# A narrow one-hot tile with its position innermost, and a bias on ScalarE in eight pieces, in an FFT and two-MoE kernel

## The chip, the cores and the metric

One core of a Trainium2 chip. The time is the device time of one execution in microseconds (us). The kernel before has a median of 3475.95 us over 3 runs.

## What is computed

The reference, cut to what matters:

```python
def reference(x, w_in, w_out, w_gate, w1, w2):
    X = np.fft.fft(np.fft.fft(x, axis=1), axis=2).real      # x: 8 x 3072 x 256
    x = X.reshape(24576, 256)
    h = x @ w_in                                            # 256 -> 2048
    x = np.where(h > 0, h, np.exp(np.minimum(h, 0)) - 1) @ w_out
    ...
    # second MoE: 24576 tokens, 8 experts, each takes exactly 3072 tokens:
    logits = x @ w_gate
    for idx in np.argsort(-logits.flatten()):               # greedy, best pair first
        tok, e = idx // 8, idx % 8
        if assigned[tok] >= 0 or counts[e] >= 3072: continue
        assigned[tok] = e; counts[e] += 1
    ...
    for e in range(8):
        out[mask_e] = np.maximum(x[mask_e] @ w1[e], 0) @ w2[e]   # 256 -> 1024 -> 256
```

## The kernel before, in words

The program has two parts. The first, `moe1`, makes the spectrum, the first MoE and the logits; it fills somewhat more than the first half of the time and the change doesn't touch it. The second, `moe2`, begins near 2000 us. It finds the order in which experts fill up, one expert after the other, and for each one does three things.

- `select(i)` finds the i-th expert to fill and the tokens that it takes, by a search over bits of the keys of the logits (lines 284 to 306) and then by counting (lines 327 to 386). A token is kept as a place: partition p of 128 and column j of 192 (NJ). The result is `ui`, the rank of each chosen token in the expert's list, which lines 393 to 401 split into `rb` (rank modulo 128) and `qb` (rank divided by 128, 0 to 23). Line 405 then adds a row of constants `cc` to all logits `L` (128 x 192 x 8), very negative for the expert that is full, and lines 408 and 409 mark its tokens as assigned. The first step of the next expert's selection, line 260, reads `L`.
- `listing(i)` turns ranks into a list of token numbers. It goes through the 192 columns in 12 pieces of 16. For a piece it makes two one-hot tiles in bf16: `oh` (line 479), 128 x 128 x 16, which is 1 where `rb` equals a given remainder; and the narrow `oq`, 128 x 48 x 16, in two halves: positions 24 to 47 are 1 where `qb` equals a given quotient (line 473), positions 0 to 23 are that times the column number (line 474), and then the upper half is scaled in place by the partition number (line 475, on ScalarE). In both tiles the column of the piece is innermost. `place` (line 452) then runs 16 matmuls, one for each column, with `oh[:, :, j]` as weights and `oq[:, :, j]` as the moving operand, so both are read with a step of 16 elements, and adds 16 results in PSUM. For experts 1 to 7 the sum is moved out after each piece (lines 457, 459); for expert 0 all 192 matmuls add into one PSUM tile, read at line 497. Line 498 makes the token numbers `idx`, and with these the rows of tokens are gathered from DRAM (line 522, on POOL's queue).
- `expert(i)` computes the expert: six groups of 512 tokens, each transposed (531), multiplied by w1 (553), split in a high and a low part on ScalarE and VectorE (565, 571), multiplied by w2 (594 to 596) and scattered (604).

The engine names are PE (TensorE), DVE (VectorE), ACT (ScalarE) and POOL (GpSimd). Each engine runs its instructions in the order in which they are written. That order comes from `ready` and from a loop that interleaves generators: while `expert(i)` is written out, steps of the next expert's `listing` and `select` are put between its matmuls, by a simple account of each engine's time (`pe`, `act`, `dve`). So for experts 1 to 7 the search and the list lie beside the previous expert's matmuls. For the first expert nothing lies beside them: `ready(0)` writes its steps in a fixed order, and there line 405 and line 474 run on POOL, where for later experts both run on DVE.

For expert 0 the tiles of the pieces come from the pool that the experts use later, so that they take no place of their own: `oh` alternates between the buffers `yh` and `yl`, the twelve `oq` are `hh0` to `hh5` and `hl0` to `hl5`. For experts 1 to 7 `oh` and `oq` have two buffers each.

Of the kernel before, what the change touches and what calls it, by code (L numbers as in the profile page):

```python
# [161 lines left out]
def moe2(tc, yd, R, w1, w2, out):  # L162
# [5 lines left out]
    with ExitStack() as ctx:  # L168
# [85 lines left out]
        def after():  # L254
            return max(ck.dve, ck.act) + AF0

        def select(i):
# [130 lines left out]
            yield after()  # L388
            while i - 1 in st and not st[i - 1]["listed"]:
                yield None  # L390
            ri = rt.tile([128, NJ], I32, name="ri")
            qi = rt.tile([128, NJ], I32, name="qi")
            nc.vector.tensor_scalar(ri, ui, 127, None, op0=OP.bitwise_and)
            nc.vector.tensor_scalar(qi, ui, 7, None, op0=OP.arith_shift_right)
# [7 lines left out]
            st[i] = dict(rb=rb, qb=qb, wix=wix, listed=False)  # L402
            dve(900)
            yield after()
            (nc.vector if i else nc.gpsimd).tensor_tensor(L, L, cc.unsqueeze(1).to_broadcast([128, NJ, E]), op=OP.add)
            dve(1700)
            yield after()
            nc.vector.scalar_tensor_tensor(u2, ui, float(CAP), fa, op0=OP.is_lt, op1=OP.mult)
            nc.vector.tensor_tensor(asg, asg, u2, op=OP.add)
            dve(600)  # L410
# [2 lines left out]
        def listing(i):  # L413
            while i not in st:
                yield None
            rb, qb, wix = (st[i][n] for n in ("rb", "qb", "wix"))
            wr = [wp.tile([128, 2 * FE], F32, name="wr%d" % a) for a in range(2)]
            for a, src in enumerate((w1.rearrange("e (p c) f -> (e p) (c f)", c=2),
                                     w2.rearrange("e (p c) d -> (e p) (c d)", c=8))):
                nc.gpsimd.indirect_dma_start(out=wr[a], out_offset=None, in_=src,  # L420
                                             in_offset=bass.IndirectOffsetOnAxis(ap=wix[:, 0:1], axis=0))
            fetched = ck.pe
            pj = small("pj", 48)
            prev = None
            while now[0] < i - 1:
                yield None
            wsp = [wp.tile([128, 2 * FE], F32R, name=n, bufs=2) for n in ("w1h", "w1l", "w2h", "w2l")]

            def split():
                for c in range(2):  # L430
                    rv = wr[0].rearrange("p (c f k) -> p c k f", c=2, k=8)[:, c]
                    hv, lv = (t.rearrange("p (c k f) -> p c k f", c=2, k=8)[:, c] for t in wsp[0:2])
                    nc.scalar.activation(hv, rv, AF.Copy)
                    (nc.gpsimd if i else nc.vector).tensor_tensor(lv, rv, hv, op=OP.subtract)
                    act(950)
                    yield after()
                for c in range(2):
                    ws = slice(1024 * c, 1024 * c + 1024)
                    nc.scalar.activation(wsp[2][:, ws], wr[1][:, ws], AF.Copy)
                    nc.gpsimd.tensor_tensor(wsp[3][:, ws], wr[1][:, ws], wsp[2][:, ws], op=OP.subtract)  # L440
                    act(950)
                    yield after()

            parts = split()

            if i == 0:
                pl0 = psum.tile([128, 48], F32, name="acc20")

            def place(c, oh, oq):
                pl = rps([128, 48]) if i else pl0  # L450
                for j in range(16):
                    nc.tensor.matmul(pl, oh[:, :, j], oq[:, :, j], start=j == 0 and (i > 0 or c == 0),  # L452
                                     stop=j == 15 and (i > 0 or c == NC - 1))
                if i == 0:
                    return
                if c:
                    nc.vector.tensor_tensor(pj, pl, pj, op=OP.add)
                else:
                    nc.vector.tensor_copy(pj, pl)

            for c in range(NC):
                js = slice(16 * c, 16 * c + 16)
                if i:
                    oh = rt.tile([128, 128, 16], BF16, name="oh", bufs=2)
                    oq = rt.tile([128, 48, 16], BF16, name="oq", bufs=2)
                else:
                    oh = ex.tile([128, 128, 16], BF16, name=("yh", "yl")[c % 2])
                    oq = ex.tile([128, 48, 16], BF16, name="h%s%d" % ("hl"[c % 2], c // 2), bufs=1)

                def row(a, n):  # L470
                    return a[:, js].unsqueeze(1).to_broadcast([128, n, 16])

                nc.vector.tensor_tensor(oq[:, 24:48], io16[:, 0:24], row(qb, 24), op=OP.is_equal)
                (nc.vector if i > 0 else nc.gpsimd).tensor_tensor(oq[:, 0:24], oq[:, 24:48], row(jb, 24), op=OP.mult)
                nc.scalar.activation(oq[:, 24:48], oq[:, 24:48], AF.Copy, scale=pcol)
                dve(750)
                act(450)
                yield 0
                nc.vector.tensor_tensor(oh, io16, row(rb, 128), op=OP.is_equal)
                if prev:  # L480
                    place(*prev)
                prev = (c, oh, oq)
                dve(1300)
                if ck.pe > fetched + WAIT:
                    next(parts, None)
                yield after()
            place(*prev)
            while ck.pe < fetched + WAIT and i and not draining[0]:
                yield None
            if i:  # L490
                yield from parts
            st[i]["listed"] = True
            while now[0] < i - 1:
                yield None
            idx = small("idx", 24, I32)
            if i == 0:
                nc.vector.tensor_copy(pj, pl0)
            nc.vector.scalar_tensor_tensor(idx, pj[:, 0:24], 128.0, pj[:, 24:48], op0=OP.mult, op1=OP.add)
            plan[i] = dict(idx=idx, wr=wr)
            plan[i]["w"] = wsp  # L500
            if i:
                ahead()
            else:
                fetch(*queue.pop(0))
                out_y[0] += 1
            dve(100)
            yield after()
            yield from parts
# [128 lines left out]
        def ready(i):  # L637
            draining[0] = True
            while i not in st:
                sel_s.step()  # L640
            if i == 0:
                for _ in range(5):
                    lst_s.step()
                sel_s.step()
            while i not in plan or "w" not in plan[i]:
                lst_s.step()
            if i == 0:
                for _ in range(1):
                    sel_s.step()
                for _ in range(2):  # L650
                    lst_s.step()
                for _ in range(2):
                    sel_s.step()
                turn(0, 0)
                for _ in range(2):
                    lst_s.step()
            draining[0] = False
            ck.pe = max(ck.pe, ck.dve - 1500)
            ahead()
# [634 lines left out]
```

## Time and profile before

| | |
|---|---|
| median of 3 runs | 3475.95 us (3472.55 to 3478.8) |
| profiled execution | 3493.99 us, of which the span is 3492.2 us |
| mean granted clock of TensorE | 0.977 of full speed |
| PE busy | 3343.3 us (96%) |
| DVE busy | 2637.7 us (76%) |
| ACT busy | 2257.5 us (65%) |
| POOL busy | 641.0 us (18%) |
| place of the first expert's list | about 2068 to 2100 us |

The span runs from the first to the last instruction of one profiled execution. That execution is 18 us longer than the median of the runs shown. Busy shares are averages over stages that have different limits. A row of a timeline gives start, duration, engine, line, operation, tiles (out<-in) and shapes; "x16" merges neighbouring instructions of one line, and the duration is then that of all of them. In brackets stands the idle time before it and what ended it.

### The profile page before, as it was taken

What the parts mean: (1) busy time and instruction counts of PE and PEld (TensorE: products, weight loads), DVE (VectorE), ACT (ScalarE), POOL (GpSimd) and SP (SyncE); (2) the same over time, 40 slices, a digit from 0 to 9 for tenths busy, and PEclk for the clock granted to TensorE, in tenths of its full rate; (3) what the DMA queues carried; (4) which work ended last, traced back from release to release, by engine and by line L of the source; (5) the groups of instructions that cost most, each with busy time, mean ns of one, the idle gap of its engine ahead of it and who ended that gap; (6) DMA issues with size and microseconds to landing.
All of it is one profiled execution on the core that took longest, in us unless ns stands there. A gap on an engine that the chain in (4) does not pass through costs nothing.

```text
span 3492.2 us, 62331 instructions
## 1 busy us (share of the span) xinstructions
PE 3343.3 (96%) x25472; PEld 3121.3 (89%) x25472; DVE 2637.7 (76%) x4930; ACT 2257.5 (65%) x3029; POOL 641.0 (18%) x837
## 2 busy tenths in 40 slices
PE   7999999999999999999999828999999999999999
PEld 4999999999999999999999827888798888888998
DVE  7888888888878888888878887677677777777522
ACT  4777777778777777777777736454546364645332
POOL 4000000000000000000000034333343334243432
PEclk9999999999999999999999958999999999999999
DMA  7112121121121111211100001111111111111110
GB/s 202 30 47 50 45 42 31 52 42 40 33 45 51 35 42 40 42 46 36 37 13 13 19 25 43 49 48 51 40 55 43 52 43 61 61 37 60 40 48 32
DMA packets 97075, 159.30 MB, mean 46 GB/s; under 512 B 18515, under 2 KB 68439, under 8 KB 94613
## 3 DMA queue, kind: packets, MB, share of 16 engines
q1 hardware_dynamic: 68357, 66.54, 7.8%
q0 software_dynamic: 24736, 80.42, 7.5%
q10 hardware_dynamic: 3696, 8.36, 0.7%
q8 instruction: 200, 3.28, 0.4%
q14 instruction: 86, 0.70, 0.1%
HBM read 91.78 MB, written 63.47 MB: 44 GB/s over the span
## 4 chain that ended last, share of the span: by engine, by line
PE 85%; DVE 6%; ACT 4%; issue 2%; DMA 1%; POOL 0%; another core or an unknown queue 0%; ACTq 0%; DVEq 0%; POOLq 0%; SPq 0%
PE hps L553 14%; PE acc L1116 11%; PE acc L1115 11%; PE acc L1114 11%; PE pq L1061 5%; PE pq L1063 5%; PE pq L1062 5%; PE acc L594 4%; PE acc L596 3%; PE acc L595 3%; PE rps L452 3%; ACT junk L289 3%; PE pq L1065 3%; PE pq L785 2%; PE pq L867 1%
## 5 line engine op out<-in xcount | busy, mean ns | idle before, releaser
L1116 PE MATMUL acc<-woh,gl 128*128 128x264 f32 x3072 | 876.1, 285 | 1.2 <-DVE gl L1101 1.1
L1115 PE MATMUL acc<-wol,gh 128*128 128x264 f32 x3072 | 875.2, 285 | 0.0
L1114 PE MATMUL acc<-woh,gh 128*128 128x264 f32 x3072 | 873.8, 284 | 1.3 <-DVE wol L1035 1.3
L1114 PEld LDWEIGHTS acc<-woh,gh 128*128 128x128 f32 x3072 | 578.9, 188 | 1.5 <-issue 1.5
L1116 PEld LDWEIGHTS acc<-woh,gl 128*128 128x128 f32 x3072 | 578.7, 188 | 1.7 <-DVE gl L1101 1.6
L1115 PEld LDWEIGHTS acc<-wol,gh 128*128 128x128 f32 x3072 | 577.8, 188 | 0.0
L1084 ACT ACTIVATE e<-h 128x1024 f32<-128x1024 f32 x384 | 408.5, 1064 | 158.5 <-DVE h L1078 158.1
L1077 DVE TENSOR_TENSOR h<-pq,qs 128x512 f32<-128x512 f32 x384 | 265.6, 692 | 287.9 <-ACT qs L1071 286.9
L1101 DVE TENSOR_TENSOR gl<-g,gh 128x1024 fp32r<-128x1024 f32 x384 | 468.4, 1220 | 1.6 <-ACT gh L1096 1.6
L1091 DVE SCALAR_TENSOR_TENSOR g<-e,h 128x1024 f32<-128x1024 f32 x384 | 467.5, 1218 | 0.1
L594 PE MATMUL acc<-w2h,hh 128*128 128x256 f32 x1536 | 455.9, 297 | 0.5 <-issue 0.4
L596 PE MATMUL acc<-w2h,hl 128*128 128x256 f32 x1536 | 435.0, 283 | 2.2 <-DVE hl L571 1.9
L595 PE MATMUL acc<-w2l,hh 128*128 128x256 f32 x1536 | 435.7, 284 | 0.0
L571 DVE SCALAR_TENSOR_TENSOR hl<-hps,hh 128x512 fp32r<-128x512 f32 x384 | 262.9, 688 | 216.6 <-ACT hh L565 195.8
L1086 ACT ACTIVATE e<-e 128x1024 f32<-128x1024 f32 x384 | 408.0, 1063 | 10.7
L1096 ACT ACTIVATE gh<-g 128x1024 fp32r<-128x1024 f32 x384 | 404.3, 1053 | 2.1 <-PE acc L1115 2.1
L1071 ACT ACTIVATE qs<-pq 128x512 f32<-128x512 f32 x384 | 230.2, 600 | 209.0 <-PE pq L1065 204.7
L565 ACT ACTIVATE hh<-hps 128x512 fp32r<-128x512 f32 x384 | 227.0, 594 | 200.1 <-PE hps L553 149.1
L604 POOL DMA_INDIRECT out<-osb,yg x192 | 203.6, 1060 | 621.6 <-ACT osb L601 591.5
L553 PE MATMUL hps<-yh,w1h 128*128 128x512 f32 x768 | 311.6, 406 | 2.0 <-DVE hl L571 1.9
L553 PE MATMUL hps<-yh,w1l 128*128 128x512 f32 x768 | 302.3, 394 | 0.0
L553 PE MATMUL hps<-yl,w1h 128*128 128x512 f32 x768 | 301.0, 392 | 0.0
(319 smaller groups left out, 7465.3 us busy)
## 6 DMA issues: line engine op xcount, KB each, us to landing
yd<-ysb SPq DMA_DIRECT2D x48, 514.0 KB
zd<-zev SPq DMA_DIRECT2D x29, 385.5 KB
xa<-x SPq DMA_DIRECT2D x28, 384.0 KB
zt<-zd SPq DMA_DIRECT2D x16, 193.5 KB
xa<-w_out ACTq DMA_DIRECT2D x6, 512.0 KB
zt<-zd SPq DMA_DIRECT2D x32, 96.0 KB
yg<-yd,idx POOLq DMA_INDIRECT x192
out<-osb,yg POOLq DMA_INDIRECT x192
```

Source lines behind the costliest of these rows:

```text
L553: nc.tensor.matmul(ps, w[:, ws], v[:, c], start=c + k == 0, stop=c + k == 3)
L594: nc.tensor.matmul(acc[t // 2][:, t % 2], hh[:, ts], w2h[:, fs], start=f == 0, stop=False)
L595: nc.tensor.matmul(acc[t // 2][:, t % 2], hh[:, ts], w2l[:, fs], start=False, stop=False)
L596: nc.tensor.matmul(acc[t // 2][:, t % 2], hl[:, ts], w2h[:, fs], start=False, stop=f == 7)
L1084: nc.scalar.activation(e, st["h"], AF.Relu, scale=-1.0)
L1086: nc.scalar.activation(st["e"], st["e"], AF.Exp, scale=-1.0)
L1091: nc.vector.scalar_tensor_tensor(g, st["e"], -1.0, st["h"], op0=OP.add, op1=OP.max)
L1096: nc.scalar.activation(st["gh"], st["g"], AF.Copy)
L1101: nc.vector.tensor_tensor(st["gl"], st["g"], st["gh"], op=OP.subtract)
L1114: nc.tensor.matmul(o, st["gh"][:, i, ts], woh(c), start=c == 0, stop=False)
L1115: nc.tensor.matmul(o, st["gh"][:, i, ts], wol(c), start=False, stop=False)
L1116: nc.tensor.matmul(o, st["gl"][:, i, ts], woh(c), start=False, stop=c == 15)
```

## The change

```diff
@@ select(i)
-            ri = rt.tile([128, NJ], I32, name="ri")
+            ri = rt.tile([128, NJ], I32, name="u1")
...
-            (nc.vector if i else nc.gpsimd).tensor_tensor(L, L, cc.unsqueeze(1).to_broadcast([128, NJ, E]), op=OP.add)
-            dve(1700)
-            yield after()
+            if i:
+                nc.vector.tensor_tensor(L, L, cc.unsqueeze(1).to_broadcast([128, NJ, E]), op=OP.add)
+                dve(1700)
+                yield after()
+            else:
+                for e in range(E):
+                    nc.scalar.activation(L[:, :, e], L[:, :, e], AF.Identity, bias=cc[:, e:e + 1])
+                    yield 0
@@ listing(i), place
-                    nc.tensor.matmul(pl, oh[:, :, j], oq[:, :, j], start=j == 0 and (i > 0 or c == 0),
+                    nc.tensor.matmul(pl, oh[:, :, j], oq[:, j], start=j == 0 and (i > 0 or c == 0),
@@ listing(i), the loop over 12 pieces
-                    oq = rt.tile([128, 48, 16], BF16, name="oq", bufs=2)
+                    oq = rt.tile([128, 16, 48], BF16, name="oq", bufs=2)
...
-                    oq = ex.tile([128, 48, 16], BF16, name="h%s%d" % ("hl"[c % 2], c // 2), bufs=1)
+                    oq = ex.tile([128, 16, 48], BF16, name="h%s%d" % ("hl"[c % 2], c // 2), bufs=1)
...
-                nc.vector.tensor_tensor(oq[:, 24:48], io16[:, 0:24], row(qb, 24), op=OP.is_equal)
-                (nc.vector if i > 0 else nc.gpsimd).tensor_tensor(oq[:, 0:24], oq[:, 24:48], row(jb, 24), op=OP.mult)
-                nc.scalar.activation(oq[:, 24:48], oq[:, 24:48], AF.Copy, scale=pcol)
+                eqq = (rt.tile([128, 24, 16], BF16, name="eqq") if i else
+                       ex.tile([128, 24, 16], BF16, name="hl7", bufs=1))
+                ov = oq.rearrange("p j q -> p q j")
+                nc.vector.tensor_tensor(eqq, io16[:, 0:24], row(qb, 24), op=OP.is_equal)
+                (nc.vector if i > 0 else nc.gpsimd).tensor_tensor(ov[:, 0:24], eqq, row(jb, 24), op=OP.mult)
+                nc.scalar.activation(ov[:, 24:48], eqq, AF.Copy, scale=pcol)
@@ ready(0)
-                for _ in range(5):
-                    lst_s.step()
-                sel_s.step()
+                for k in range(E):
+                    for _ in range(2):
+                        lst_s.step()
+                    sel_s.step()
```

The narrow tile becomes 128 x 16 x 48: the position is innermost, and the moving operand `oq[:, j]` of a matmul is 48 elements in a row. The comparison no longer goes into the tile itself but into a tile `eqq` of one buffer (`hl7` of the experts' pool for expert 0, so order rows of expert 0 call it `hl`), and the multiply and the scaling both read it and write into `oq` with a step of 48 elements. `oh` stays as it was. For expert 0 the addition to the logits leaves POOL and becomes eight activations on ACT, one for each expert's column of the logits, written one after each of the first eight pieces. `ri` shares the buffer of `u1`.

In the changed file the lines are 481 (comparison), 482 (multiply), 483 (scaling), 487 (`oh`), 457 (matmul) and 411 (the new activation).

DVE's order in the first expert's list, with the engines that each instruction waits for in brackets. Before:

```order
L473 TENSOR_TENSOR hh_24162<-io_23598,qb 128x384 [waits DMAHW1_49,DMAHW7_49,DMAHW0_49,DVE_49]
L479 TENSOR_TENSOR yh<-io_23598,rb 128x2048 [waits Activation_49]
L473 TENSOR_TENSOR hl_24168<-io_23598,qb 128x384
L479 TENSOR_TENSOR yl<-io_23598,rb 128x2048
L473 TENSOR_TENSOR hh_24190<-io_23598,qb 128x384
```

Changed:

```order
L481 TENSOR_TENSOR hl_24163<-io_23598,qb 128x384 [waits DMAHW1_49,DMAHW7_49,DMAHW0_49,DVE_49]
L487 TENSOR_TENSOR yh<-io_23598,rb 128x2048 [waits Activation_49]
L481 TENSOR_TENSOR hl_24171<-io_23598,qb 128x384 [waits Activation_49,Pool_49]
L487 TENSOR_TENSOR yl<-io_23598,rb 128x2048
L481 TENSOR_TENSOR hl_24195<-io_23598,qb 128x384 [waits Activation_49,Pool_49]
```

The order is the same; from the second piece on the comparison waits for ACT and POOL, which read `eqq` of the piece before.

ACT's order at the same place. Before:

```order
L400 ACTIVATE rb<-ri 128x192 [waits DVE_49]
L475 ACTIVATE hh_24162<-hh_24162,pcol 128x384 [waits DMAHW3_49,DMAHW1_49,DMAHW7_49,DMAHW0_49,Pool_49]
L475 ACTIVATE hl_24168<-hl_24168,pcol 128x384 [waits Pool_49]
L475 ACTIVATE hh_24190<-hh_24190,pcol 128x384 [waits Pool_49]
L475 ACTIVATE hl_24213<-hl_24213,pcol 128x384 [waits Pool_49]
```

Changed:

```order
L400 ACTIVATE rb<-u_24143 128x192 [waits DVE_49]
L483 ACTIVATE hh_24162<-hl_24163,pcol 128x24x16 [waits DMAHW3_49,DMAHW1_49,DMAHW7_49,DMAHW0_49,DVE_49]
L411 ACTIVATE L<-L,cc 128x192 [waits DMAHW3_49]
L483 ACTIVATE hl_24170<-hl_24171,pcol 128x24x16 [waits DVE_49]
L411 ACTIVATE L<-L,cc 128x192
```

The scaling waits for DVE's comparison and no longer for POOL's multiply, and between the scalings of the first eight pieces stand the eight additions to the logits. On POOL line 405, which stood between the third and the fourth multiply, is gone.

DVE's order in the lists of experts 1 to 7. Before:

```order
L473 TENSOR_TENSOR oq<-io_23598,qb 128x384 [waits DVE_49]
L474 TENSOR_TENSOR oq<-oq,jb 128x384 [waits DVE_49]
L479 TENSOR_TENSOR oh<-io_23598,rb 128x2048
L473 TENSOR_TENSOR oq<-io_23598,qb 128x384
L474 TENSOR_TENSOR oq<-oq,jb 128x384 [waits DVE_49]
```

Changed:

```order
L481 TENSOR_TENSOR eqq<-io_23598,qb 128x384 [waits DVE_49]
L482 TENSOR_TENSOR oq<-eqq,jb 128x24x16 [waits DVE_49]
L487 TENSOR_TENSOR oh<-io_23598,rb 128x2048
L481 TENSOR_TENSOR eqq<-io_23598,qb 128x384 [waits DVE_49,Activation_49]
L482 TENSOR_TENSOR oq<-eqq,jb 128x24x16 [waits DVE_49]
```

Here too the order stays, and the comparison of the second piece waits for ACT's scaling of the first. On PE the order of all instructions is the same in both kernels.

## Rows read from the trace of the kernel before

**Rows 1.** The page, busy time, share and instructions of each engine

```profile
PE 3343.3 (96%) x25472; PEld 3121.3 (89%) x25472; DVE 2637.7 (76%) x4930; ACT 2257.5 (65%) x3029; POOL 641.0 (18%) x837
```

**Rows 2.** By stretch: busy PE, PEld, DVE, ACT, POOL, granted clock, DMA, GB/s

```profile
2068.00:2100.00 32.00, 20.39 (x192) 19.00 (x192) 28.62 (x28) 10.03 (x14) 25.67 (x14) 0.50 0.09 32
2550.00:2630.00 80.00, 79.96 (x593) 72.04 (x593) 59.45 (x113) 35.22 (x53) 34.29 (x35) 1.00 0.17 56
```

**Rows 3.** The same for line 452 alone: busy PE, PEld, clock, DMA, GB/s

```profile
2550.00:2630.00 80.00, 20.75 (x192) 18.25 (x192) 1.00 0.17 56
```

**Rows 4.** Line 452: count: duration ns min/median/max, first and last start, forms

```profile
L452 PEld LDWEIGHTS <-oh x1344: 142/148/180, 2216.4 to 3278.4; 128*128 128x128 bf16 x192
L452 PE MATMUL rps<-oq,oh x1344: 267/279/306, 2216.4 to 3278.5; 128*128 128x48 bf16 x192
L452 PE MATMUL acc<-hh,yh x96: 255/279/288, 2070.7 to 2096.7; 128*128 128x48 bf16 x96
L452 PE MATMUL acc<-hl,yl x96: 255/278/288, 2072.8 to 2098.9; 128*128 128x48 bf16 x96
```

**Rows 5.** Timeline of PE, a run of 16 in the list of expert 2

```profile
2399.49 1.74 PE L452 MATMUL rps<-oq,oh 128*128 128x48 bf16 x16
```

**Rows 6.** Contiguous bf16 operands, lines 342, 376: by source, then timeline of PE

```profile
L342 PEld LDWEIGHTS <-gm x96: 95/96/106, 2060.4 to 3206.4; 128*128 128x128 bf16 x96
L342 PE MATMUL rps<-wb,gm x96: 169/169/183, 2062.5 to 3206.4; 128*128 128x16 bf16 x96
...
L376 PE MATMUL rps<-trij,tots x32: 243/245/368, 2064.9 to 3210.5; 96*128 96x192 bf16 x32
...
2199.56 0.44 PE L342 MATMUL rps<-wb,gm 128*128 128x16 bf16 x12 [0.28 <-DVE sgn L335]
```

**Rows 7.** First list, one run: timeline of PE, then line 452 by stretch

```profile
2095.30 1.70 PE L452 MATMUL acc<-hh,yh 128*128 128x48 bf16 x16 [0.44 <-ACT hh L475]
...
2095.29:2095.37 0.08, 0.07 (x1) 0.07 (x1) 0.50 0.00 0
2095.29:2095.38 0.09, 0.08 (x2) 0.08 (x2) 0.50 0.00 0
```

**Rows 8.** Timeline of DVE and of POOL, first pieces of the first list

```profile
2067.74 0.36 DVE L473 TENSOR_TENSOR hh<-io,qb 128x384 bf16<-128x384 bf16 x1
2068.02 1.22 DVE L479 TENSOR_TENSOR yh<-io,rb 128x2048 bf16<-128x2048 bf16 x1
2069.16 1.07 DVE L473 TENSOR_TENSOR hl<-io,qb 128x384 bf16<-128x384 bf16 x1
2071.28 1.07 DVE L473 TENSOR_TENSOR hh<-io,qb 128x384 bf16<-128x384 bf16 x1
...
2068.24 1.76 POOL L474 TENSOR_TENSOR hh<-hh,jb 128x384 bf16<-128x384 bf16 x1 [2.74 <-ACT rb L400]
```

**Rows 9.** The same around line 405, POOL and then DVE

```profile
2074.23 3.59 POOL L405 TENSOR_TENSOR L<-L,cc 128x1536 f32<-128x1536 f32 x1
...
2074.41 4.49 DVE L479 TENSOR_TENSOR yl<-io,rb 128x2048 bf16<-128x2048 bf16 x1
```

**Rows 10.** Line 400, an activation of 192 elements

```profile
L400 ACT ACTIVATE rb<-ri x1: 364/364/364, 2067.3 to 2067.3; 128x192 bf16<-128x192 int32 x1
```

**Rows 11.** End of the first list: timeline of POOL, ACT and PE

```profile
2094.89 1.84 POOL L474 TENSOR_TENSOR hl<-hl,jb 128x384 bf16<-128x384 bf16 x1 [0.29 <-DVE hl L473]
...
2096.76 0.62 ACT L475 ACTIVATE hl<-hl,pcol 128x384 bf16<-128x384 bf16 x1 [1.52 <-POOL hl L474]
...
2097.43 1.72 PE L452 MATMUL acc<-hl,yl 128*128 128x48 bf16 x16 [0.43 <-ACT hl L475]
```

**Rows 12.** Line 474 on DVE, experts 1 to 7

```profile
L474 DVE TENSOR_TENSOR oq<-oq,jb x84: 357/358/3140, 2214.8 to 3270.8; 128x384 bf16<-128x384 bf16 x84
```

**Rows 13.** Timeline of ACT and DVE, first two pieces of expert 1

```profile
2215.21 0.62 ACT L475 ACTIVATE oq<-oq,pcol 128x384 bf16<-128x384 bf16 x1 [2.75 <-DVE oq L474]
...
2216.23 0.35 DVE L473 TENSOR_TENSOR oq<-io,qb 128x384 bf16<-128x384 bf16 x1
```

## The prediction

> **What bounds the kernel now.** I read the totals first. TensorE (PE) is busy 96% of the span and VectorE (DVE) 76% [rows 1], but an average over stages prices no change, so next I cut the span around the lines that the change touches. They stand in two stages with different limits. In the 32 us in which the list of the first expert is made, PE is busy 20 us at a granted clock of 0.50, the lower of its two levels (1.2 GHz), while DVE is busy 28.6 and POOL 25.7 [rows 2]: a chain of DVE and POOL sets the time there. In a stretch in which a later expert's list is made, PE is busy 79.96 of 80 us at the full clock, DVE 59 of 80 [rows 2]: there PE alone sets the time, and of those 80 us the placing matmuls of line 452 take 20.75 [rows 3]. So what the new tile does for PE counts seven times, for experts 1 to 7, and what it does elsewhere counts once.
>
> **The placing matmuls.** There are 1344 in those seven lists (84 runs of 16) and 192 for the first expert [rows 4]. One run of 16 takes 1.74 us; less the 0.28 of the last matmul, and over 15 spacings, that is 97 ns from one to the next [rows 4, 5]. Is it the 48 moving columns or the 128 weight columns that cost this? Both are read with a step of 16 elements, and the change makes only the moving side contiguous.
>
> The moving side: matmuls with contiguous bf16 operands take 169 ns for 16 columns, 244 to 245 for 192 [rows 6], so some 163 plus 0.42 per column; 48 columns would take 183. The shortest of line 452 take 255 [rows 4]. They stand in the first expert's list, where PE waits for ACT before each run, so that the first matmul of a run finds its weights loaded: this is no wait for weights. So 48 stepped columns cost about 92 ns beyond the fixed 163, some 1.9 ns each, close to the spacing of 97. And the spacing is 97 at either level of the clock (1.70 and 1.74 us per run [rows 5, 7]). I take it that the moving read sets the spacing.
>
> The weight side, which stays: a stepped load takes 148 ns, a contiguous one of the same size 96 [rows 4, 6], so 52 ns more. Contiguous pairs follow each other at (0.44 - 0.169) / 11 = 25 ns [rows 6]; with the 52 on top a pair whose weights alone are stepped would take 77. A second reading comes from the start of a run in the first list, where the first matmul has its weights and the second waits for a stepped load that begins with the first: the second begins 70 to 80 ns later, since one has begun by 2095.37 and two by 2095.38 [rows 7]. I take 74 for the new spacing. The gain is 97 - 74 = 23 ns, and 23 x 1344 = 30.9 us, on PE's own path. Ends: 0 if the weight load needs all of the 97, and (97 - 25) x 1344 = 97 us if a stepped load hides as a contiguous one does.
>
> By the Trainium skill (TensorE: Matmul & The Clock Gate, section LDWEIGHTS) a weight load takes its columns over 1.2 ns, so 107 ns for 128; by that rule the load would keep the spacing where it is and this term would be zero. The rows speak against it, since pairs with 128 weight columns follow each other every 25 ns [rows 6]; it stays as a rival.
>
> **The first expert's list.** Today a piece runs thus [rows 8]: DVE compares (line 473, 0.36 us when nothing disturbs it), then makes the wide tile (479, 1.21); POOL's multiply (474) begins at 2068.24 and ends at 2070.00, and all but about 0.78 of it lies beside the end of line 479; the next compare, issued at 2069.16, ends 0.23 after POOL. DVE and POOL hold each other up here, and a piece takes 2.12 to 2.13 us (2069.16 to 2071.28).
> - *Line 405 leaves POOL.* It takes 3.59, and line 479 beside it takes 4.49 in place of 1.21 [rows 9]. Gain 3.3 us.
> - *Eight ScalarE pieces come.* An activation of 192 elements takes 0.36 [rows 10]. ACT is busy 10 of 32 us in this stage [rows 2], idle for 22, and nobody in the list waits for them: the reader of the logits, line 260, comes after the list. Cost 0, covered by that idle time; without that cover 8 x 0.36 = 2.9.
> - *DVE's compare now waits for POOL and ACT*, because there is one tile eqq. It already ended after POOL; now it starts after POOL. A piece becomes 0.28 (compare to wide tile) + 1.21 + 0.78 + about 0.06 for the signal = 2.33, so 0.20 more, 11 times: 2.2 us lost. Behind it on DVE stands the wide tile, for which PE waits.
> - *POOL now writes with a step of 96 bytes.* No row shows this. Lower end 0, since nothing suggests a gain. Line 405, of four-byte elements, takes 3.59 / 1536 = 2.3 ns each, line 474 about 0.78 / 384 = 2.0. I take this difference, 0.12 per piece, 1.4 us in all, as that row is nearest; upper end, an extra for each element as large as PE's stepped read, 384 x 1.9 ns = 0.73 per piece, 8.8 in all.
> - *The end of the list.* Today the last multiply, ACT's 0.62 and PE's 1.72 follow in series [rows 11]. ACT now reads eqq and not POOL's result, so its 0.65 with the signal goes, and the last run of 16 shortens by 15 x 0.023 plus about 0.08 of its last matmul. Gain 1.1.
>
> Sum of this stage: -3.3 + 2.2 + 1.4 - 1.1 = -0.8 us.
>
> The Trainium skill (GPSIMD Engine Reference, section Performance pitfalls for Q7 kernels) has a price for stepped reads only, about half more per element; if a stepped write paid as much, POOL would cost 0.39 x 12 = 4.7 us here, and the stage would come to +2.5.
>
> **Experts 1 to 7, beside PE.** DVE's multiply takes 0.36 for 384 elements [rows 12]; no row shows it with a stepped write. Lower end 0 more, upper end the same 0.73 more: 84 x 0.73 = 61 us over seven stretches, 9 in each, in which DVE has 20 of 80 us idle [rows 2]. Cost 0; without that cover DVE would reach PE's level and the gain would go. The new wait of the compare for ACT: I set the end of each ACT scaling (0.62) against the start of the next compare. The smallest distances are about 0.40, as in [rows 13]; of 77 only three are under 1 us. Cost 0, covered by these distances. Without them hl of the experts (line 571), which stands behind the compare on DVE, would be late, and PE waits for hl. Moving ri into u1's tile costs nothing: DVE writes and reads both in its own order, and u1's last reader comes before ri.
>
> **Sum.** -30.9 - 0.8 = -31.7 us against the profiled execution, whose time is 3494.0: 3462.3. The runs shown have a median of 3476.0, 18 us lower, so for the median I forecast 3476 - 31.7 = 3444 us.
>
> **The rivals.**
> - *The weight load sets the spacing, and the new tile gives PE nothing.* For it: the load is stepped too and lasts 148 ns. Against it: the 255 ns of matmuls that had their weights. It is where the rule on weight loads of the Trainium skill's page named above would lead. The time would be 3476 - 0.8 = 3475. Chance 0.14.
> - *The stepped load hides better than I take it.* For it: its excess may be latency. At a spacing of 43 ns, between 25 and 60, the gain is 54 x 1344 = 73 us, time 3402. Chance 0.18.
> - *The gain is partly given back*: DVE's multiply with a stepped write delays hl, for which PE waits. With half the gain gone, 3460. Against it: those 20 idle us in 80. Chance 0.06.
> - *Slower: POOL's stepped write* in the first list. Each microsecond more per piece costs 12 us, with nothing beside it. To lose 7 us in all against my other terms, it must take 0.9 + (31.7 + 7) / 12 = 4.1 us in place of 0.8, over 10 ns an element; at 5 us the time is 3476 - 31.7 + 49 = 3493. For it: the whole of POOL's step lies on the path there. Against it: nothing in the rows comes near that price. Chance 0.03.
>
> **How the numbers follow.** My forecast, spacings of 60 to 90 ns, has the remaining 0.59; it covers 3426 to 3466. The second rival reaches to 3402 and below; I let the range begin at 3404 and end at 3475, which leaves out half of that rival, part of the first and the last one, about 2 in 10. A measurement here can tell some 0.2%, 7 us, from no change. Faster by more than that: the forecast, the second and third rival, and 0.02 of the first, 0.85. Same: 0.12. Slower: 0.03.
>
> **What would show it.** Right: runs of 16 placing matmuls of about 1.3 us with matmul durations near or below 255 ns and weight loads still near 148; no POOL operation over the logits and no wide tile of 4.5 us; pieces of the first list of about 2.4 us; no wait of PE that is new in experts 1 to 7. A spacing still at 97 with short matmuls proves the weights to be the limit; pieces of 3 us or more, POOL's write.

## The result and the profile after

The changed kernel takes 3523.07 us (median of 4 runs, 3522.60 to 3528.39) against 3476.59 for the kernel before beside it: a ratio of 1.0138 (95% interval 1.0121 to 1.0156), 46.5 us slower. The forecast was 3444, faster; the time lies above its whole range.

Sets of runs differ a little: the kernel before takes 3475 to 3477 us in three of the four sets used here and 3491 in one, about the gap between the profiled execution and the median ahead of the prediction. What makes this difference isn't known; the record gives the same chip number to the set of 3491 and to one of the others. So spans are subtracted only between profiles of one set, and the sets are compared by their ratios to the kernel before. The rows below are from such a pair (`before_here` and `after_again` among the experiments): spans 3475.0 and 3517.5, 42.5 us apart.

The page of the changed kernel, busy time as in [rows 1] and the engines' shares of the chain that ended last:

```profile
PE 3311.8 (94%) x25472; PEld 3079.8 (88%) x25472; DVE 2761.3 (79%) x4930; ACT 2389.7 (68%) x3037; POOL 668.2 (19%) x836
...
PE 77%; DVE 12%; ACT 6%; issue 2%; POOL 1%; DMA 1%; ACTq 0%; DVEq 0%; POOLq 0%
```

The same of the kernel before, from its page in this pair:

```profile
PE 3338.3 (96%) x25472; PEld 3116.4 (90%) x25472; DVE 2636.1 (76%) x4930; ACT 2254.2 (65%) x3029; POOL 640.3 (18%) x837
...
PE 86%; DVE 6%; ACT 4%; issue 2%; DMA 1%; POOL 1%; ACTq 0%; DVEq 0%; POOLq 0%; SPq 0%
```

PE has 27 us less work, DVE 125 and ACT 135 us more, and the chain moves from PE to DVE and ACT. Two parts make up the 42.5. The first expert's list, from the first comparison to `idx`, grows from 31.7 to 42.2 us. The rest, from the first w1 matmul of expert 0 to the end, grows from 1363.1 to 1395.1, by 32.0.

**The first list.** Timeline of the changed kernel (481 is the comparison, 482 the multiply, 483 the scaling, 487 the wide tile, 457 the matmuls), to be held against [rows 7, 8, 11]:

```profile
2067.70 0.36 DVE L481 TENSOR_TENSOR hl<-io,qb 128x384 bf16<-128x384 bf16 x1
2067.97 1.22 DVE L487 TENSOR_TENSOR yh<-io,rb 128x2048 bf16<-128x2048 bf16 x1
2068.09 2.11 ACT L483 ACTIVATE hh<-hl,pcol 128x384 bf16<-128x384 bf16 x1 [0.50 <-DVE hl L481]
2068.20 2.86 POOL L482 TENSOR_TENSOR hh<-hl,jb 128x384 bf16<-128x384 bf16 x1 [2.74 <-ACT rb L400]
...
2071.09 0.36 DVE L481 TENSOR_TENSOR hl<-io,qb 128x384 bf16<-128x384 bf16 x1 [1.90 <-POOL hh L482]
2071.11 1.13 PE L457 MATMUL acc<-hh,yh 128*128 128x48 bf16 x16 [5.38 <-POOL hh L482]
...
2074.49 0.36 DVE L481 TENSOR_TENSOR hl<-io,qb 128x384 bf16<-128x384 bf16 x1 [1.90 <-POOL hl L482]
...
2109.90 0.18 DVE L506 SCALAR_TENSOR_TENSOR idx<-pj 128x24 int32<-128x24 f32 x1
```

A piece takes 3.40 us (2071.09 to 2074.49) in place of 2.13. DVE is done with the wide tile at 2069.19 and then idles 1.90 us for POOL, whose multiply ends at 2071.06, 1.87 after the wide tile. Before, it ended 0.78 after it [rows 8].

**The later lists.** The stretch of a list runs from about its first comparison to its last `pj`. Busy time by stretch of the changed kernel: the first list, those of experts 2 and 4, then the sum over the lists of experts 1 to 7 (columns as in [rows 2]):

```profile
2068.11:2109.68 41.57, 13.62 (x192) 13.85 (x192) 17.55 (x24) 30.55 (x22) 35.03 (x12) 0.50 0.06 24
...
2392.77:2464.50 71.73, 60.48 (x490) 52.66 (x488) 66.40 (x78) 42.55 (x40) 23.85 (x19) 1.00 0.09 33
...
2732.53:2808.86 76.33, 66.88 (x520) 59.40 (x519) 71.11 (x78) 43.44 (x41) 28.21 (x23) 0.93 0.11 39
...
sum 489.15, PE 432.63 PEld 380.24 DVE 454.21 ACT 297.33 POOL 208.48; mean PE 61.80 PEld 54.32 DVE 64.89 ACT 42.48 POOL 29.78
```

The same of the kernel before, expert 2 and the sum:

```profile
2382.46:2447.81 65.35, 65.31 (x497) 59.57 (x495) 47.09 (x76) 27.15 (x40) 21.28 (x19) 1.00 0.11 42
...
sum 461.64, PE 455.65 PEld 415.43 DVE 323.38 ACT 189.11 POOL 190.41; mean PE 65.09 PEld 59.35 DVE 46.20 ACT 27.02 POOL 27.20
```

In the list of expert 2 PE has 4.8 us less to do, yet the stretch is 6.4 us longer. PE was busy in all of it, now in 84%; DVE went from 72 (47.09 of 65.35) to 93% (66.40 of 71.73). DVE has taken PE's place as the bound. Instructions of the touched lines of the changed kernel by source (count: shortest, median, longest, ns), which answer to [rows 4, 10, 12]:

```profile
L457 PEld LDWEIGHTS <-oh x1344: 141/167/175, 2223.5 to 3303.5; 128*128 128x128 bf16 x192
L457 PE MATMUL rps<-oq,oh x1344: 218/220/278, 2223.5 to 3303.5; 128*128 128x48 bf16 x192
...
L482 DVE TENSOR_TENSOR oq<-eqq,jb x84: 1970/2034/9814, 2220.4 to 3297.4; 128x384 bf16<-128x384 bf16 x84
L482 POOL TENSOR_TENSOR hh<-hl,jb x6: 2857/2924/2942, 2068.2 to 2102.1; 128x384 bf16<-128x384 bf16 x6
...
L483 ACT ACTIVATE oq<-eqq,pcol x84: 2105/2162/2244, 2220.4 to 3297.4; 128x384 bf16<-128x384 bf16 x84
...
L411 ACT ACTIVATE L<-L,cc x8: 872/882/885, 2069.7 to 2093.5; 128x192 f32<-128x192 f32 x8
```

The matmuls are shorter, as wanted. But DVE's multiply takes 2.03 us where it took 0.36 [rows 12], and ACT's scaling 2.16 where it took 0.62 [rows 13]: both now write with a step of 96 bytes. What PE waits for after 2150 us (us in total, times, longest), first in the changed kernel, then in the kernel before:

```profile
PE hps L561 <- DVE hl L579: 22.8, 15, 6.2
PE rps L457 <- DVE pj L462: 11.2, 6, 3.5
PE rps L271 <- DVE pj L462: 10.5, 4, 4.2
PE acc L604 <- DVE hl L579: 9.2, 7, 6.0
PE tps L539 <- DMA yg<-yd,idx: 7.7, 6, 4.2
```

```profile
PE tps L531 <- DMA yg<-yd,idx: 7.8, 6, 4.2
PE hps L553 <- DVE hl L571: 1.8, 3, 1.2
PE rps L452 <- DVE pj L457: 1.7, 1, 1.7
PE acc L596 <- DVE hl L571: 1.6, 1, 1.6
...
PE rps L271 <- DVE pj L457: 0.8, 1, 0.8
```

The wait for the gather is as before; the waits for `hl` and `pj` went from some 6 to 54 us. One of them, in the timeline of the list of expert 2:

```profile
2458.60 2.00 DVE L482 TENSOR_TENSOR oq<-eqq,jb 128x384 bf16<-128x384 bf16 x1
2458.66 2.13 ACT L483 ACTIVATE oq<-eqq,pcol 128x384 bf16<-128x384 bf16 x1 [0.77 <-DVE eqq L481]
...
2460.49 0.39 PE L561 MATMUL hps<-yl,w1h 128*128 128x512 f32 x1
2461.24 0.69 DVE L579 SCALAR_TENSOR_TENSOR hl<-hps,hh 128x512 fp32r<-128x512 f32 x1 [0.65 <-ACT hh L573]
2461.85 1.22 DVE L487 TENSOR_TENSOR oh<-io,rb 128x2048 bf16<-128x2048 bf16 x1
2462.98 0.20 DVE L462 TENSOR_TENSOR pj<-rps,pj 128x48 f32<-128x48 f32 x1
...
2463.24 0.93 PE L457 MATMUL rps<-oq,oh 128*128 128x48 bf16 x12 [2.36 <-DVE pj L462]
```

PE is through at 2460.88. `hh` stands behind ACT's scaling, `hl` behind DVE's multiply and `hh`, the wide tile behind `hl`, and `pj`, for which PE waits, behind that: 2.36 us idle.

The 32.0 us add up so: PE idles 51.0 us more after the first w1 matmul (27.1 to 78.1), the runs of placing matmuls take 42.2 less (122.7 to 80.5, first to last start of each of the 84), and the remaining 23 lie with matmuls that last longer. Most of that is the clock: the granted level is the lower one, 1.2 GHz, for 53.6 us of this part, 14.8 before. At that level the w1 matmuls of the trace follow each other every 427 ns, at the upper one every 227, so 38.8 us more of it put PE up to 18 us behind, an estimate. In the list of expert 4 (0.93 in the third row above) the clock fell at 2756, just after PE had waited 2.60 us for `hl`.

### The profile page after: what moved, and what is told of

It reads as the page before. It is cut to its first block, busy times and chain, and to the rows that moved or that the text cites. A ratio compares the mean times of both kernels' runs of the same rounds, so it can differ in the third digit from the quotient of the medians.

```text
span 3521.2 us, 62355 instructions
## 1 busy us (share of the span) xinstructions
PE 3320.7 (94%) x25472; PEld 3086.2 (88%) x25472; DVE 2761.1 (78%) x4930; ACT 2390.2 (68%) x3037; POOL 667.4 (19%) x836
## 4 chain that ended last, share of the span: by engine, by line
PE 78%; DVE 12%; ACT 6%; issue 2%; POOL 1%; DMA 1%; ACTq 0%; DVEq 0%; POOLq 0%
PE hps L561 12%; PE acc L1125 11%; PE acc L1124 11%; PE acc L1123 11%; PE pq L1070 5%; PE pq L1072 5%; PE pq L1071 5%; PE acc L602 3%; ACT junk L289 3%; PE pq L1074 3%; PE acc L604 3%; PE acc L603 2%; DVE oq L482 2%; PE pq L794 2%; DVE oh L487 1%
## 5 line engine op out<-in xcount | busy, mean ns | idle before, releaser
L561 PE MATMUL hps<-yh,w1h 128*128 128x512 f32 x768 | 318.8, 415 | 21.3 <-DVE hl L579 20.8
L612 POOL DMA_INDIRECT out<-osb,yg x192 | 212.8, 1108 | 616.3 <-ACT osb L609 592.6
```

Of the source, the lines that this page charges most:

```text
L561: nc.tensor.matmul(ps, w[:, ws], v[:, c], start=c + k == 0, stop=c + k == 3)
```

## The experiments

Two theories stood against each other. **The stepped writes** on DVE, ACT and POOL cost the time, by holding those engines longer. Or **something else in the change** does: the one buffer of `eqq`, or the eight pieces on ACT. The trace of the changed kernel already speaks against the buffer for the later lists: DVE sits idle before line 481 for POOL alone, 20.9 us in all, all of it in the first list, and nowhere for ACT. Every kernel computes the whole result.

**The layout undone on the writers' side, in steps.** Four kernels in one set of runs (before: 3476.91). `no_step` has `eqq` position-innermost too:

```diff
-eqq = rt.tile([128, 24, 16], ...)
+eqq = rt.tile([128, 16, 24], ...)
-nc.vector.tensor_tensor(eqq, io16[:, 0:24], row(qb, 24), op=OP.is_equal)
+nc.vector.tensor_tensor(eqq, jb[:, 0:24].unsqueeze(1).to_broadcast([128, 16, 24]), col(qb), op=OP.is_equal)
-(...).tensor_tensor(ov[:, 0:24], eqq, row(jb, 24), op=OP.mult)
+(...).tensor_tensor(oq[:, :, 0:24], eqq, col(jb), op=OP.mult)
-nc.scalar.activation(ov[:, 24:48], eqq, AF.Copy, scale=pcol)
+nc.scalar.activation(oq[:, :, 24:48], eqq, AF.Copy, scale=pcol)
```

where `col(a)` repeats a column's value over 24 positions. `both_read_step` leaves `eqq` and the comparison as the change has them, and multiply and scaling read it with a step of 16 elements (`ez`, its rearranged view) and write runs of 24. `mul_write_step` keeps the stepped write on the multiply alone, `scale_write_step` on the scaling alone:

```diff
 # mul_write_step
-nc.scalar.activation(ov[:, 24:48], eqq, AF.Copy, scale=pcol)
+nc.scalar.activation(oq[:, :, 24:48], ez, AF.Copy, scale=pcol)
 # scale_write_step
-(...).tensor_tensor(ov[:, 0:24], eqq, row(jb, 24), op=OP.mult)
+(...).tensor_tensor(oq[:, :, 0:24], ez, col(jb), op=OP.mult)
```

> The new tile as in the change, but eqq is laid out 16 x 24 like the tile, and the comparison, the multiply and the scaling all run with the position innermost, so that each writes runs of 24 neighbouring elements; nothing is written or read there with a step. Engines, buffers and waits are those of the change. Theory W (the stepped writes of the change, 2.03 us on DVE and 2.14 on ACT per piece, ate what PE gained): the placing matmuls keep the changed kernel's spacing of 60 ns in place of 97, 37 x 1344 = 50 us less on PE, no PE wait for hl or pj beyond that of before, multiply and scaling near 0.6 us; time 3415 to 3435. Rival S (the single eqq tile, DVE waiting for ACT before each comparison, is what costs): it is still there, so 3500 or more.

> The change, with the multiply and the scaling iterating so that they write runs of 24 elements and read eqq with a step of 16 elements (32 bytes) in place of writing with a step of 96 bytes. Theory W: a stepped write is dear and a stepped read is not, so multiply and scaling come to 0.4 to 0.8 us and the time to 3415 to 3440. Rival 'any step is dear': DVE and ACT stay near 2 us per piece, and the time near 3523.

> The change, with the stepped write left on the multiply alone (DVE for experts 1 to 7, POOL for the first); the scaling on ACT writes runs of 24. Theory W-DVE (it is DVE's 84 x 1.67 = 140 us more, on the engine that was busy three quarters, for which PE waits by hl and pj): 3505 to 3523. Rival W-ACT (it is ACT's 84 x 1.5 = 128 us more, which makes hh late and so hl): the experts' loss is gone, and only the first list's 10 us stays on top of the gain, 3430 to 3445.

> The change, with the stepped write left on ACT's scaling alone; the multiply (DVE for experts 1 to 7, POOL for the first) writes runs of 24. Theory W-DVE: 3415 to 3440. Rival W-ACT: 3500 to 3520.

Measured: `no_step` 3451.67 (ratio 0.9924, 0.9907 to 0.9940), `both_read_step` 3459.54 (0.9951, 0.9934 to 0.9967), `scale_write_step` 3483.08 (1.0017, 1.0007 to 1.0027), `mul_write_step` 3507.45 (1.0087, 1.0070 to 1.0104). Multiply and scaling of each, by source, in the order `no_step`, `both_read_step`, `mul_write_step`, `scale_write_step`:

```profile
L484 DVE TENSOR_TENSOR oq<-eqq,jb x84: 557/558/6070, 2209.2 to 3229.9; 128x384 bf16<-128x384 bf16 x84
...
L485 ACT ACTIVATE oq<-eqq,pcol x84: 606/616/619, 2209.2 to 3229.9; 128x384 bf16<-128x384 bf16 x84
```

```profile
L486 DVE TENSOR_TENSOR oq<-eqq,jb x84: 841/903/6546, 2209.4 to 3236.7; 128x384 bf16<-128x384 bf16 x84
...
L487 ACT ACTIVATE oq<-eqq,pcol x84: 981/1047/1126, 2209.4 to 3236.8; 128x384 bf16<-128x384 bf16 x84
```

```profile
L486 DVE TENSOR_TENSOR oq<-eqq,jb x84: 1971/2040/9968, 2218.5 to 3284.9; 128x384 bf16<-128x384 bf16 x84
...
L487 ACT ACTIVATE oq<-eqq,pcol x84: 993/1051/1115, 2218.5 to 3285.0; 128x384 bf16<-128x384 bf16 x84
```

```profile
L486 DVE TENSOR_TENSOR oq<-eqq,jb x84: 846/898/4451, 2211.4 to 3259.9; 128x384 bf16<-128x384 bf16 x84
...
L487 ACT ACTIVATE oq<-eqq,pcol x84: 2105/2171/2253, 2211.4 to 3260.0; 128x384 bf16<-128x384 bf16 x84
```

An instruction that keeps the stepped write lasts over 2 us; one that only reads with a step lasts 0.90 or 1.05, whatever the other does. Medians, less `both_read_step`: a stepped write in place of a stepped read costs 47.9 us on DVE and POOL, 23.5 on ACT. Of the 47.9 the first list takes 11.8 (30.5 to 42.3 us, 0.98 a piece). Together with the 7.9 by which `both_read_step` stands above `no_step`, the parts come to 79.3, where `no_step` and the change are 71.4 apart. The interval of such a ratio reaches up to 6 us to either side, so an overlap of the parts isn't shown; nothing beyond them is needed. `no_step` is faster than both kernels.

By their expectations, rival S falls, and so does "any step is dear". Neither W-DVE nor W-ACT is right alone: `mul_write_step` lies where W-DVE put it, `scale_write_step` between the two. `no_step` and `both_read_step` came out some 17 and 20 us above the theory's upper ends. The first had counted all that PE gains, and where that goes is said below; in the second, multiply and scaling also last longer than the 0.4 to 0.8 us expected.

**The other parts of the change, each alone.** Four kernels in the set of runs where the kernel before takes 3490.87. `bias_alone` is the kernel before with the eight pieces on ACT and the new order in `ready(0)`; `tile_alone` is the change without these; `two_eqq` is the change with `eqq` in two buffers:

```diff
-eqq = rt.tile([128, 24, 16], BF16, name="eqq")
+eqq = rt.tile([128, 24, 16], BF16, name="eqq", bufs=2)
-       ex.tile([128, 24, 16], BF16, name="hl7", bufs=1)
+       ex.tile([128, 24, 16], BF16, name=("hl7", "hh7")[c % 2], bufs=1)
```

> The kernel before, unchanged, for a second profile: its first profile stands 18 us above its median, the changed kernel's at its median. If the extra is chance of that execution, the second profile lies within 5 us of 3477, and its experts' part (from the first matmul of line 553 to the end, 1380 us in the first profile) within 1358 to 1370. If the profiler itself slows this program, it is near 3494 again.

> The kernel before with one part of the change alone: the first expert's constants go to the logits in eight pieces on ACT, and the steps of ready(0) are those of the change; the tile stays as it was. Theory: line 405 held POOL and with it DVE's wide tile, 3.3 us, and the eight pieces (0.88 us each in the changed kernel, in place of the 0.36 of the forecast) lie in ACT's idle time: 3.3 us less, 3471 to 3476. Rival: ACT's pieces delay the scaling for which PE waits at the end, and nothing is won: 3477.

> The change without its second part: the narrow tile of the change, with the logits' constants added in one operation on POOL as before. Theory: the first list's pieces are a chain over POOL, so POOL's 3.6 us come on top of the changed kernel's time: 3525 to 3530. Rival (the eight ACT pieces cost the changed kernel something): at or under 3523.

> The change with two buffers for eqq in place of one (qi takes m's place to make room), so that a comparison no longer waits for the multiply and the scaling of the piece before. Theory W (the writes' own duration costs): the experts' part stays within 5 us of the change; in the first list POOL alone sets the piece, with the wide tile of DVE still in its way, so 3.1 to 3.4 us per piece in place of 3.40; time 3515 to 3523. Rival S (the wait for the single buffer costs): DVE no longer stands behind ACT, time under 3505.

Measured: `before_again` 3490.79 (1.0000, 0.9989 to 1.0010), `bias_alone` 3489.86 (1.0000, 0.9991 to 1.0010), `tile_alone` 3540.37 (1.0145, 1.0128 to 1.0162), `two_eqq` 3531.05 (1.0118, 1.0101 to 1.0135). The expectations in us were set against 3477, so the ratios are what counts here. The second profile is near the first again (3492.5 for 3494.0), but not because the profiler slows the program: in this set the runs that weren't profiled take 3491 too. The experts' part differs by 15 us between the two sets for the same kernel (1378 to 1363).

The tile makes the loss, not the eight pieces. These shorten the first list by 3.2 us (31.7 to 28.5); in the whole that is 0.1%, which the interval of `bias_alone` neither shows nor excludes. Two buffers bring the first list from 42.2 to 34.2 (a piece from 3.40 to 2.67), since DVE no longer waits for POOL. Against the change only ratios can be compared, and their intervals overlap. But `tile_alone` ran in the same set: from it to `two_eqq` the first list is 10.9 us shorter (45.1 to 34.2) and the median 9.3 us lower, so most of what the list gains by the second buffer and the eight pieces together does reach the end. The loss of the later lists stays.

**DVE's time without a stepped write.** If the stepped write hurts by holding DVE, any other work of that length must do the same. `mul_four_times` is `no_step` with three more multiplies in experts 1 to 7, into the same place. `no_step_two` is `no_step` with two buffers for `eqq`. The changed kernel and the kernel before were profiled beside them, the pair shown above.

```diff
 (...).tensor_tensor(oq[:, :, 0:24], eqq, col(jb), op=OP.mult)
+for _ in range(3 if i else 0):
+    nc.vector.tensor_tensor(oq[:, :, 0:24], eqq, col(jb), op=OP.mult)
```

> The kernel with runs of 24 everywhere (0.992 of before), but in the lists of experts 1 to 7 DVE does the multiply four times in a row into the same place, each without a stepped write: 4 x 0.56 = 2.2 us in place of the changed kernel's 2.03, so DVE gets about the same 1.67 us more for each of 84 pieces and POOL, ACT and PE get nothing more. Theory 'the time on DVE is what costs': PE waits longer for hl and pj, the clock falls in the list stretches, and the time rises by 30 to 50 us over the kernel with runs of 24, to a ratio of 1.001 to 1.007 of before. Rival 'it is the stepped write itself, by what it does to other engines' accesses': three short multiplies more fit in DVE's idle time and the ratio stays at 0.992 to 0.995.

> The kernel with runs of 24 everywhere, with two buffers for the compared tile, so that a comparison no longer waits for POOL and ACT of the piece before. Theory: POOL's 1.74 us and the wait behind it still chain the first list at some 2.4 us a piece; with two buffers the piece falls to about 2.1 and the first list by 2 to 4 us from 30.7; in experts 1 to 7 nothing changes. Ratio 0.990 to 0.993. Rival: as with the changed kernel's tile, what the first list gains does not reach the end, ratio 0.992 or a little above.

> The changed kernel once more, beside the kernel before on the same chip, so that their profiles can be set side by side: ratio 1.013 to 1.0155, the first list about 10.5 us longer, the rest after it about 31 us longer.

> The kernel before, profiled on the same chip as the other three: first list 32 us, nothing else new. It gives the spans to subtract.

Measured against 3475.39: `mul_four_times` 3535.65 (1.0170, 1.0153 to 1.0187), `no_step_two` 3450.49 (0.9925, 0.9909 to 0.9942), `after_again` 3523.92 (1.0141, 1.0124 to 1.0157), `before_here` 3476.76. The added multiplies of `mul_four_times`, by source; then its stretches, expert 2 and the sum; then its waits of PE:

```profile
L486 DVE TENSOR_TENSOR oq<-eqq,jb x252: 557/558/3149, 2210.3 to 3319.6; 128x384 bf16<-128x384 bf16 x126
```

```profile
2390.99:2464.75 73.76, 63.07 (x484) 54.62 (x482) 70.87 (x111) 25.86 (x38) 22.47 (x19) 0.95 0.08 29
...
sum 514.33, PE 442.48 PEld 387.29 DVE 490.63 ACT 184.83 POOL 188.79; mean PE 63.21 PEld 55.33 DVE 70.09 ACT 26.40 POOL 26.97
```

```profile
PE hps L565 <- DVE hl L583: 27.7, 17, 4.5
PE rps L457 <- DVE pj L462: 17.8, 13, 3.6
PE acc L608 <- DVE hl L583: 12.8, 5, 7.4
```

It loses 84 us against `no_step`, more than the 30 to 50 expected, with the same waits for `hl` and `pj`. So time on DVE alone is enough for such a loss, and the rival's 0.992 to 0.995 falls. Nor do the medians show that DVE's stepped write holds ACT: the stepped scaling lasts 2.16 us beside it and 2.17 without it. `mul_four_times` loses more than the change because DVE has more to do in a piece: 0.55 + 4 x 0.56 = 2.78 us for comparison and multiplies, in place of 0.35 + 2.03 = 2.38. The sums over the seven lists, from the same view of each kernel:

| kernel | sum of the 7 stretches, us | PE busy | DVE busy | ACT busy |
|---|---|---|---|---|
| before | 461.6 | 455.7 | 323.4 (70%) | 189.1 (41%) |
| `no_step` | 437.9 | 422.1 | 357.9 (82%) | 187.7 (43%) |
| `both_read_step` | 444.9 | 423.6 | 371.1 (83%) | 221.7 (50%) |
| `scale_write_step` | 463.9 | 426.2 | 374.1 (81%) | 300.7 (65%) |
| `mul_write_step` | 476.2 | 429.6 | 451.8 (95%) | 219.3 (46%) |
| changed | 489.2 | 432.6 | 454.2 (93%) | 297.3 (61%) |
| `mul_four_times` | 514.3 | 442.5 | 490.6 (95%) | 184.8 (36%) |

At 93 to 95% DVE sets the length of a stretch: from the change to `mul_four_times` 36.4 us more on DVE make 25.2 us more time. `scale_write_step` shows the other way to lose: no engine is full, but `hh` stands behind a scaling of 2.17 us on ACT, `hl` behind `hh`, and 19 us go (444.9 to 463.9); the w1 matmuls wait 18.4 us for `hl`, in `both_read_step` 8.3. The change loses both ways: with DVE as busy as in `mul_write_step` (454.2 and 451.8) its stretches are 13.0 us longer.

`no_step_two` gains 1.9 us in the first list (30.4 to 28.5) and nothing that can be measured in the whole. The profiles add up as expected of `after_again`: 10.5 us in the list, 32.0 after it.

## Why the prediction was wrong

**The step that failed is the price of the stepped write**, which the prediction said no row showed. It bounded it by PE's stepped read, 1.9 ns an element, and took 0.12 us a piece on POOL and "Cost 0" on DVE. Measured, per element of 384 and over the unstepped price: DVE (2.034 - 0.358) / 384 = 4.4 ns, ACT (2.16 - 0.62) / 384 = 4.0 ns, POOL (1.87 - 0.78, the part after the wide tile) / 384 = 2.8 ns. Each lies above what was taken as the upper end: a read on another engine was no bound for a write.

- *DVE in experts 1 to 7.* The upper end was 61 us over the seven stretches, 9 in each, "covered" by 20 idle of 80. By the mean durations over these lists (2.29 us, before 0.39) it was 84 x 1.90 = 160 us, 23 in each, more than the cover. The sentence on what comes without the cover was right: DVE reaches PE's level, `hl` is late, and PE waits for it.
- *ACT's scaling was not priced at all.* It was carried along at 0.62 us although its output has the same step as the multiply's. 84 x 1.54 = 129 us more on ACT, in front of `hh`; alone, in place of a stepped read, it costs 23.5 us.
- *POOL in the first list*: 1.4 us taken, 8.8 as the upper end, 11.8 measured between `both_read_step` and `mul_write_step`.

A row that bears on this was not weighed. The Trainium skill (Vector Engine (DVE) Microarchitecture Reference, section Measured stream behaviour on trn2) lists 2.50 ns per column where a destination of four-byte words alone steps by 24 words for every element; that is this step of 96 bytes. Worked out as an estimate, 384 x 2.50 = 0.96 us against 0.36: in the right direction, and less than half of the 2.03 that the trace shows for two-byte elements. The Trainium skill's rule that was weighed, half more per element for POOL's stepped reads (GPSIMD Engine Reference, section Performance pitfalls for Q7 kernels), doesn't carry over to writes: POOL's part after the wide tile went to 2.4 times.

**What held.**
- *Placing matmuls.* The moving read set the spacing. Runs of 16 take 1.13 to 1.18 us, a spacing of 64 ns where 74 was forecast and 97 stood before. The gain is 42.2 us by the starts in the trace, not 30.9: 33.5 ns in each of the 15 spacings of 84 runs (the forecast took 16). The size came from two readings, and the second was wrong: with the loads stepped as before, the second matmul of a run in the first list now begins 25 ns after the first, so the 70 to 80 ns of [rows 7] were no wait for a load. The fit of [rows 6], 183 ns for 48 contiguous columns, was near: the shortest of the first list now last 196. The first rival, the weight load, fell with the spacing. By the rule of the Trainium skill (TensorE: Matmul & The Clock Gate, section LDWEIGHTS) 107 ns would have remained. The loads themselves even last 167 ns each, beside other loads and matmuls.
- *Line 405 leaving POOL*: 3.3 forecast, 3.2 measured in the list. *The wait of the comparison*: 2.2 forecast, 1.9 by `no_step_two`. Without stepped writes a piece takes 2.41 us, where 2.33 came out of the sum. *The eight pieces* last 0.88 us, not 0.36, and no cost shows all the same: in `bias_alone`, at 0.66 each, the list is shorter by what line 405 took.
- *The comparison's wait for ACT in the later lists* costs nothing, as its "Cost 0" said: DVE sits idle before none of them for ACT, though the scaling grew to 2.16 us, and `two_eqq` is no faster after the first list than `tile_alone` (1416.9 and 1411.2 us, one profile each).

**The rivals.** The third (DVE's stepped multiply delays `hl`) and the fourth (POOL's stepped write in the first list) named the right mechanisms, with chances of 0.06 and 0.03. Each was argued down by its size, from the same unmeasured price, so they were not independent: one wrong price brought both at once, and ACT's with them. The range had no case for that.

**Where the gain of `no_step` goes.** PE's pace gives 42 us, the whole gains 25 (ratio 0.9924), 1.3 of it in the first list. Compared with the kernel before, PE idles 9.2 us more after the first w1 matmul (36.3 for 27.1) and stands at the lower clock 18.6 us longer (33.4 for 14.8; up to 9 us by the estimate made above). DVE is at 82% of the list stretches there, which may be why; that isn't shown. The step of `oh`, the weights, which may set the 64 ns that are left, was not tried.

## What to carry to other kernels

A layout that is good for the reader is paid for by the writers: before giving the matmul contiguous rows, look at what each engine that fills the tile then writes, and keep the inner step of every output at one element, even where that costs a little at the comparison (0.55 us for 0.35 here). An operation without a row in the trace has no "covered" cost; bound it by a row of the same kind on the same engine, or put its chance of being several times dearer into the range, in every place where it stands at once. Idle time of an engine covers new work only as far as nothing that the bound waits for stands behind it in that engine's order.

## What had not been expected of the hardware

- A write of two-byte elements with a step of 96 bytes makes DVE's multiply 5.6 times as long (2.03 for 0.36 us), ACT's scaling 3.5 times (2.16 for 0.62). A read with a step of 32 bytes, with contiguous runs written, costs far less: 0.90 for 0.56 us on DVE, 1.05 for 0.62 on ACT.
- An activation of 192 four-byte elements, read and written with a step of 32 bytes, takes 0.88 us in the changed kernel, between scalings with a stepped write; in `bias_alone` and `no_step`, where no scaling has one, it takes 0.63 to 0.69. The contiguous one, from int32 to bf16, takes 0.36 [rows 10].
- The spacing of 64 ns is nearly the same at the lower clock (60 in the first list), and the weight loads got longer, from 148 to 167 ns, as the pairs moved together.
- A DVE multiply that begins beside a row of POOL's subtractions can last as long as they do. Timeline of the changed kernel, DVE and then POOL:

```profile
2764.87 9.81 DVE L482 TENSOR_TENSOR oq<-eqq,jb 128x384 bf16<-128x384 bf16 x1
...
2765.16 3.08 POOL L439 TENSOR_TENSOR w1l<-wr,w1h 128x1024 fp32r<-128x1024 f32 x1
2768.21 4.65 POOL L445 TENSOR_TENSOR w2l<-wr,w2h 128x1024 fp32r<-128x1024 f32 x2
```

The multiply ends 1.8 us after POOL's last; PE waits 5.95 us for the `hl` behind it. Five of the 84 multiplies overlap such operations of POOL, and they are the five that last 4.1 to 9.8 us. The kernel before has the same kind of delay in its multiplies (3.14 us at most [rows 12]), and in its comparisons (up to 5.89 us).
